# One operation for both halves of a state product, over four array tiles and two PSUM banks

## The chip, the cores and the metric

The kernel runs on one core of one Trainium2 chip. The metric is device time in microseconds (us). Before the change the median of three runs is 1085.53 us; the three lie from 1074.02 to 1090.18 us.

## What is computed

The first stage is a recurrent attention over 4 batches, 8 heads, 768 steps and head size 40. Its output, 3072 rows of 320, goes through two dense blocks.

```python
for t in range(S):
    y[:, :, t] = np.einsum('bhd,bhde->bhe', rt, state)
    Sa = np.einsum('bhde,bhe->bhd', state, at)
    state_decay = state * wt[:, :, None, :] - np.einsum('bhd,bhe->bhde', Sa, bt)
    state = state_decay + np.einsum('bhd,bhe->bhde', vt, kt)
...
h = np.maximum(np.maximum(x @ w1, x @ w2), x @ w3)
x = h @ w_out
...
return (x @ w_a) * (x @ w_b) @ w_out2
```

## The kernel before

**The work.** The 768 steps are cut into 24 chunks of 32, and the chunks into 12 pairs. `prep(p)` makes a pair's decay products (L396, L400), scaled keys (L404), and the inverse of a small triangular matrix (`solve`, on VectorE and GpSimd, with round trips through DRAM whose last ones are the transfers TT<-TD and NB<-ED). `chain(c)` carries the state through one chunk, on TensorE in this order:

- `z` (L618), the chunk's right-hand sides from the old state; ScalarE copies the result out (L624);
- `h` (L632) and `u` (L645), the two steps of the triangular solution. Each has 32 matmuls of 32 by 32 by 40, on four array tiles in turn (partitions 32j of the operands to partitions 32j of the result). `h` needs TT, `u` needs NB. ScalarE copies `u`'s result into the tile XX in four pieces (L655) and into XU (L656);
- the **state product** `smm` (L665), which this change touches. It has two halves, x = 0 and x = 1. A half's operands lie in partitions 64x to 64x+63 of the tiles YR (keys) and XX (values); its 16 matmuls (8 values of u, 2 of g) write to partitions 64g to 64g+39 of one PSUM bank. So a half uses two array tiles, g = 0 and g = 1, in turn, and each half has a bank of its own;
- in chunks 1 to 8 each half stands behind a **held product** (L673): a matmul with the identity that puts the old state into the bank first, so that ScalarE only copies the sum out (L679). In the other chunks VectorE adds the bank to the state tile ST (L682). Every fourth chunk VectorE then also scales ST (L686). ScalarE copies the new state into ZR (L693), from which the next `z` reads. The last chunk has no state product;
- transposes (L578, L594, L699), `g` (L711) and `y` (L729), which make the chunk's outputs.

float32 matmuls such as these show as two MATMUL rows each in the profile; the matmuls of the dense blocks show as one.

When a pair's outputs are there, `moe_a(p)` runs the first dense block on them (L837, eight matmuls to an operation, and L862 to L866). After the last pair, `moe_b` runs the second dense block (L991 to L1001).

**What sets the order.** All of this is given to a planner (`Plan`) as operations with an estimated duration, the tiles that each reads and writes, a priority and the number of PSUM banks that it takes (`ps`). The planner places the operations one by one on the engines, and the order that results is the program of each engine; an engine then works through its own program in that order. An operation can only be placed when as many of the eight banks are free as it names. The state product's entries are 0.82 for each half, with an activity (`act`) of 0.22. The planner also keeps a model of how busy TensorE is and where it finds too little work it puts in **fillers**, 128-column matmuls with the identity into a free bank (L277) whose result nobody reads. They serve to keep TensorE's clock up.

Of the kernel before, what the change touches and what calls it, by code (L numbers as in the profile page):

```python
# [17 lines left out]
NCH = S // C  # L18
# [7 lines left out]
NACC = 9  # L26
# [23 lines left out]
class Plan:  # L50
# [8 lines left out]
    def op(self, eng, dur, fn, r=(), w=(), ps=(), fin=(), pri=0.0, lat=None, after=(), pre=0.0, cls=0, alt=(), act=1.0, bias=None):  # L59

        i = len(self.ops)
        deps = set(after)
        for k in r:
            if k in self.lw:
                deps.add(self.lw[k])
        for k in w:
            if k in self.lw:
                deps.add(self.lw[k])
            deps.update(self.rd.get(k, ()))
        for k in r:  # L70
            self.rd.setdefault(k, []).append(i)
        for k in w:
            self.lw[k] = i
            self.rd[k] = []
        deps.discard(i)
        ways = {eng: (dur, fn, 0.0)}
        ways.update({e: (d, f, bias if bias is not None else 0.0 if pri < BIASP else BIAS) for e, d, f in alt})
        self.ops.append(dict(i=i, ways=ways, bias=bias, deps=deps, ps=tuple(ps), fin=tuple(fin), pri=pri, lat=lat, pre=pre, cls=cls, act=act))
        return i
# [159 lines left out]
def body(nc, tc, ia, out_ap):  # L239
    from contextlib import ExitStack  # L240

    V, A, G, T, SP = nc.vector, nc.scalar, nc.gpsimd, nc.tensor, nc.sync
    es = ExitStack()
    P = Plan(8)
    op = P.op
    npair = NP

    def dv(n, ps=False):
        return 0.15 + n * 0.00105 if ps else 0.12 + n * 0.0014

    def ac(n):
        return 0.17 + n * 0.0009
# [14 lines left out]
    bank = [psp.tile([128, 512], F32, name=f"bank{i}") for i in range(8)]  # L267
# [7 lines left out]
    con = cst.tile([128, 192], F32, name="con")  # L275
    ident = con[:, 0:128]
# [40 lines left out]
    ST = ap_.tile([128, 8, 2, 64], F32, name="ST")  # L317
# [223 lines left out]
    def chain(c):  # L541
        p, cc = divmod(c, 2)
        b, kb_ = p % NPB, p % 2
        z, z2, yb = c % NZR, (c + 1) % NZR, c % NYR
        pr = 0.001 * c
# [27 lines left out]
        for hf in range(2):  # L573
            pn = ("a", "yt", c, hf)
# [7 lines left out]
            for x in range(2):  # L582
# [3 lines left out]
                   r=[pn], w=[("YRy", yb, x, hf)], fin=[pn] if x else (), pri=0.5 + 0.001 * c)  # L586

        if c:
            for hf in range(2):
                pn = ("a", "st", c, hf)  # L590
# [7 lines left out]
                for i in range(2):  # L598
# [3 lines left out]
                       r=[pn], w=[("YRs", yb, 1 - i, hf)], pri=0.3 + 0.001 * c)  # L602
# [3 lines left out]
                       r=[pn], w=[("YRs2", yb, 1 - i, hf)], fin=[pn] if i else (), pri=0.3 + 0.001 * c)  # L606
# [3 lines left out]
        def zmm(w_):  # L610
# [11 lines left out]
           r=[(k, b, g, cc) for k in ("Za", "Zk") for g in range(2)] + [("ZRs", z, g) for g in range(2)] + [("ZRv", z, g) for g in range(2)],  # L622
           w=[pz], ps=[pz], pri=pr)
# [31 lines left out]
                own.append(op("ACT", ac(320), lambda w_, o_=o_, i_=i_: A.activation(o_(), i_(w_), AF.Copy), r=[pu], w=[("XXu", x, pq)], pri=pr))  # L655
        op("ACT", ac(320), lambda w_: A.activation(XU.rearrange("p b g d -> p (b g d)"), bank[w_[pu]][:, 0:320], AF.Copy), r=[pu], w=["XU"], fin=[pu], pri=pr, after=own)  # L656

        for x in range(2):
            pn = ("a", "s", c, x)

            def smm(w_, early, x=x, pn=pn):
                ps = bank[w_[pn]]
                for u in range(8):
                    for g in range(2):
                        T.matmul(ps[64 * g:64 * g + 40, u * 40:u * 40 + 40],  # L665
                                 Y_[64 * x:64 * x + 64, x, u, g], XX[64 * x:64 * x + 64, u, g], start=not early, stop=True, skip_group_check=early)

            if c == NCH - 1:
                continue
            early = 0 < c < NACC  # L670
            if early:

                op("PE", 0.6, lambda w_, x=x, pn=pn: T.matmul(bank[w_[pn]][0:104, 0:320], ident[0:104, 0:104], ST[0:104, :, 1 - x, 0:40], start=True, stop=False, skip_group_check=True),  # L673
                   r=["ST", ("STx", x), "con"], w=[pn], ps=[pn], act=0.9, pri=pr)
            op("PE", 0.82, lambda w_, smm=smm, early=early: smm(w_, early), r=[("YRy", yb, x, hf) for hf in range(2)] + [("XXu", x, pq) for pq in range(2)] + [("XXv", x)],
               w=[pn], ps=[] if early else [pn], act=0.22, pri=pr)
            sv = ST[0:104, :, 1 - x, 0:40]
            if early:
                op("ACT", ac(320), lambda w_, sv=sv, pn=pn: A.activation(sv, bank[w_[pn]][0:104, 0:320].rearrange("p (u d) -> p u d", d=40), AF.Copy),  # L679
                   r=[pn], w=["ST", ("STx", x)], fin=[pn], pri=pr)  # L680
            else:
                op("DVE", dv(320, True), lambda w_, sv=sv, pn=pn: V.tensor_tensor(  # L682
                    sv, bank[w_[pn]][0:104, 0:320].rearrange("p (u d) -> p u d", d=40), sv, ALU.add),
                   r=[pn], w=["ST", ("STx", x)], fin=[pn], pri=pr)
            if cc and p % 2:
                op("DVE", 0.74, lambda w_, sv=sv, x=x: V.tensor_tensor(  # L686
                    sv, sv, P_[0:104, cc].rearrange("p (u x) s -> p u x s", x=2)[:, :, x, 32:33].to_broadcast([104, 8, 40]), ALU.mult),
                   r=pc, w=["ST", ("STx", x)], pri=pr)
            for g in range(2):
                r0 = GP[g]  # L690
                o_ = ZR[z2][r0:r0 + 40, g, :, 1 - x]
                i_ = ST[r0:r0 + 40, :, 1 - x, 0:40]
                op("ACT", ac(320), lambda w_, o_=o_, i_=i_: A.activation(o_, i_, AF.Copy), r=[("STx", x)], w=[("ZRs", z2, g)], pri=pr)  # L693
# [3 lines left out]
        def xtr(w_):  # L697
# [6 lines left out]
            r=[px], w=[("XTu", 0), ("XTu", 1)], fin=[px], pri=0.2 + pr)  # L704
# [9 lines left out]
        for x in range(2):  # L714
# [4 lines left out]
               r=[pg, "con"], w=[("YLg", x)], fin=[pg] if x else (), pri=0.2 + pr)  # L719
        py = ("a", "y", c)  # L720

        def ymm(w_):
# [14 lines left out]
           r=[py] + pc, w=[("XY", cc), "cxa", "cxb", "cxf"], fin=[py], pri=0.2 + pr)  # L737
# [305 lines left out]
    for p in range(npair):  # L1043
        a0 = len(P.ops)
        chain(2 * p)
        chain(2 * p + 1)
        if p + 2 < npair:
            prep(p + 2)
        gather(p)
        att.extend(range(a0, len(P.ops)))  # L1050
        a0 = len(P.ops)
        moe_a(p)
        ma.extend(range(a0, len(P.ops)))
# [218 lines left out]
```

## Time and profile before

| what | us |
|---|---|
| runs, lowest / median / highest | 1074.02 / 1085.53 / 1090.18 |
| span of the profiled execution, first to last instruction | 1092.1 |
| TensorE busy in it | 1045.6 (96%) |
| VectorE busy | 639.8 (59%) |
| ScalarE busy | 499.3 (46%) |

The profiled execution has no time of its own beside its span; it is 6.6 us above the median of the runs and 1.9 us above the highest. Engines: PE is TensorE's matmuls, PEld its weight loads, DVE VectorE, ACT ScalarE, POOL GpSimd, SP the engine that issues most transfers. PEclk is the share of TensorE's full clock that was granted; the clock has two levels, 1.2 and 2.4 GHz, so 0.90 over a stretch means a fifth of it at the lower level. A busy PE is not one at its peak: a pipelined matmul's row is longer than the time until the next one starts.

### The profile page before, as it was taken

The numbers are of one execution on the slowest core, as the hardware profiler recorded it, in microseconds if no ns is written. First come the engines' busy times: TensorE is split into PE (matmuls) and PEld (weight loads), VectorE is DVE, ScalarE is ACT, GpSimd is POOL, SyncE is SP. The second block draws the span as 40 slices with busy tenths as digits, with TensorE's granted clock in tenths as the row PEclk, the third lists the DMA queues.
The fourth block names the chain that finished last, engine by engine and source line by source line (L and its number), as shares of the span: only waits on it lengthen the run. The fifth ranks groups of instructions, "written<-read, shape, count | busy, mean of one in ns | idle before, by whom it ended". The sixth has DMA issues, their size and how long they took to land.

```text
span 1092.1 us, 34136 instructions
## 1 busy us (share of the span) xinstructions
PE 1045.6 (96%) x14792; PEld 938.5 (86%) x14792; DVE 639.8 (59%) x1035; ACT 499.3 (46%) x1157; POOL 252.2 (23%) x212
## 2 busy tenths in 40 slices
PE   8999799999989999899999999999999999999997
PEld 7888687878889888789899999988888888888886
DVE  7796797696778787787877333376223232332222
ACT  5357664576656467474756522243222232222221
POOL 3332555343336625441413000011000000000000
PEclk9899896989999989999999999999999999999999
DMA  8757874867666677857555239522002000000000
GB/s 266 178 128 165 184 171 105 175 138 189 171 165 169 151 167 199 184 134 184 132 140 131 55 103 274 131 78 61 22 1 54 1 25 1 1 25 1 25 1 27
DMA packets 173436, 123.08 MB, mean 113 GB/s; under 512 B 122464, under 2 KB 147168, under 8 KB 172320
## 3 DMA queue, kind: packets, MB, share of 16 engines
q1 hardware_dynamic: 170688, 116.41, 43.3%
q10 hardware_dynamic: 2592, 4.42, 1.1%
q8 instruction: 118, 1.93, 0.8%
q14 instruction: 38, 0.31, 0.1%
HBM read 93.07 MB, written 27.72 MB: 111 GB/s over the span
## 4 chain that ended last, share of the span: by engine, by line
PE 56%; DVE 2%; DMA 2%; issue 1%; SPq 1%; ACT 0%; POOL 0%; ACTq 0%; DVEq 0%; POOLq 0%
PE bank L991 24%; PE bank L837 10%; PE bank L999 4%; PE bank L1000 4%; PE bank L1001 4%; PE bank L665 1%; PE bank L862 1%; PE bank L729 1%; PE bank L711 1%; PE bank L864 1%; PE bank L863 1%; PE bank L594 1%; PE bank L645 1%; PE bank L632 1%; PE bank L429 1%
## 5 line engine op out<-in xcount | busy, mean ns | idle before, releaser
L1009 DVE TENSOR_TENSOR bas<-bank,bas 128x512 f32<-128x512 f32 x72 | 49.8, 691 | 194.1 <-PE bank L991 185.3
L991 PE MATMUL bank<-bxhi,bw 128*128 128x512 f32 x576 | 156.3, 393 | 0.0
L991 PEld LDWEIGHTS bank<-bxhi,bw 128*128 128x128 f32 x576 | 106.0, 188 | 20.6
L1008 ACT ACTIVATE bas<-bank 128x512 f32<-128x512 f32 x72 | 43.0, 598 | 143.1 <-PE bank L991 143.0
L1011 ACT ACTIVATE bgh<-bas 128x512 fp32r<-128x512 f32 x72 | 45.6, 633 | 132.4 <-DVE bas L1009 132.4
L837 PE MATMUL bank<-xhi,whi 128*128 128x256 f32 x432 | 97.6, 309 | 0.2 <-issue 0.2
L991 PE MATMUL bank<-bxlo,bw 128*128 128x512 f32 x288 | 89.7, 393 | 0.0
L837 PE MATMUL bank<-xhi,wlo 128*128 128x256 f32 x432 | 89.6, 290 | 0.0
L837 PE MATMUL bank<-xlo,whi 128*128 128x256 f32 x432 | 89.3, 289 | 0.0
L999 PE MATMUL bank<-bo,bgh 128*128 128x320 f32 x288 | 88.9, 309 | 0.0
L1001 PE MATMUL bank<-bo,bgl 128*128 128x320 f32 x288 | 88.9, 309 | 0.0
L1000 PE MATMUL bank<-bo,bgh 128*128 128x320 f32 x288 | 88.8, 308 | 0.0
L852 DVE TENSOR_TENSOR hm<-bank,hm 128x512 f32<-128x512 f32 x72 | 49.5, 687 | 63.3 <-PE bank L837 59.7
L414 POOL TENSOR_TENSOR ZL<-ZL,Pp 64x512 f32<-64x512 f32 x44 | 59.8, 1360 | 88.6 <-DVE Pp L396 69.9
L1012 DVE TENSOR_TENSOR bgl<-bas,bgh 128x512 fp32r<-128x512 f32 x72 | 50.7, 705 | 42.8 <-ACT bgh L1011 42.6
L837 PEld LDWEIGHTS bank<-xhi,whi 128*128 128x128 f32 x432 | 68.9, 198 | 5.3 <-DVE wraw L760 1.6
L837 PEld LDWEIGHTS bank<-xhi,wlo 128*128 128x128 f32 x432 | 69.8, 198 | 0.0
L837 PEld LDWEIGHTS bank<-xlo,whi 128*128 128x128 f32 x432 | 69.8, 198 | 0.0
L991 PEld LDWEIGHTS bank<-bxlo,bw 128*128 128x128 f32 x288 | 54.1, 188 | 12.3
L837 PE MATMUL bank<-xt,wt 128*128 128x256 f32 x216 | 62.3, 288 | 0.8 <-issue 0.8
L837 PE MATMUL bank<-xl,wt 128*128 128x256 f32 x216 | 62.1, 287 | 0.0
L277 PE MATMUL bank<-con 128*128 128x128 f32 x386 | 57.2, 301 | 3.4 <-DMA con<-in_con_dram 2.8
(183 smaller groups left out, 2488.5 us busy)
## 6 DMA issues: line engine op xcount, KB each, us to landing
wraw<-in_wpb_dram SPq DMA_DIRECT2D x18, 480.0 KB
KT<-in_kb_dram SPq DMA_DIRECT2D x20, 384.0 KB
Pp<-in_wf_dram SPq DMA_DIRECT2D x10, 528.0 KB
Rp<-in_wr_dram SPq DMA_DIRECT2D x10, 528.0 KB
wraw<-in_wpa_dram SPq DMA_DIRECT2D x12, 384.0 KB
bw<-WD SPq DMA_DIRECT2D x9, 512.0 KB
WD<-wraw ACTq DMA_DIRECT2D x18, 240.0 KB
WD<-wca SPq DMA_DIRECT2D x18, 240.0 KB
```

What stands on the lines that cost most here:

```text
L277: P.keep = lambda b: T.matmul(bank[b][:, 0:128], ident, ident, start=True, stop=True)
L414: op("POOL", po(512), lambda w_, cc=cc, g=g, r0=r0: G.tensor_tensor(Z_[r0:r0 + 64, cc, g], Z_[r0:r0 + 64, cc, g], P_[r0:r0 + 64, cc, :, 0: ...
L837: T.matmul(ps, w, x, start=(i == 0), stop=(i == 7))
L852: op("DVE", dv(512, True), lambda w_, pn=pn: V.tensor_tensor(f(hm), bank[w_[pn]], f(hm), ALU.max), r=[pn], w=["hm"], fin=[pn], pri=ep)
L991: T.matmul(ps, w, x, start=(k == 0), stop=(k == 7))
L999: T.matmul(o, gh[:, c], oh, start=ff == 0, stop=False)
L1000: T.matmul(o, gh[:, c], ol, start=False, stop=False)
L1001: T.matmul(o, gl[:, c], oh, start=False, stop=ff == 11)
L1008: op("ACT", ac(512), lambda w_, j=j, pa=pa: A.activation(tb["as", j], bank[w_[pa]], AF.Copy), r=[pa], w=[("bas", j)], fin=[pa], pri=ep)
L1009: op("DVE", dv(512, True), lambda w_, j=j, pb=pb: V.tensor_tensor(tb["as", j], bank[w_[pb]], tb["as", j], ALU.mult), r=[pb], w=[("bas", j) ...
L1011: op("ACT", ac(512), lambda w_, j=j, k=k: A.activation(tb["gh", k], tb["as", j], AF.Copy), r=[("bas", j)], w=[("gh", k)], pri=ep)
L1012: op("DVE", dv(512), lambda w_, j=j, k=k: V.tensor_tensor(tb["gl", k], tb["as", j], tb["gh", k], ALU.subtract), r=[("bas", j), ("gh", k)], ...
```

## The change

The two halves become one operation of 32 matmuls. Its loops run over u, then x, then g, so that consecutive matmuls go to (x, g) = (0,0), (0,1), (1,0), (1,1): four array tiles in turn, the x = 0 ones into the first bank and the x = 1 ones into the second. It reads what both halves read, and takes both banks at once. The two held products become one operation as well. What the planner is told changes: 0.9 for the whole product with an activity of 0.4, and 1.2 for both held products. The copies and sums behind it (L679 to L693) stay one per half; lines from L679 on are two higher in the changed kernel.

```diff
-        for x in range(2):
-            pn = ("a", "s", c, x)
-
-            def smm(w_, early, x=x, pn=pn):
-                ps = bank[w_[pn]]
-                for u in range(8):
+        pss = [("a", "s", c, x) for x in range(2)]
+        early = 0 < c < NACC
+
+        def smm(w_):
+            for u in range(8):
+                for x in range(2):
                     for g in range(2):
-                        T.matmul(ps[64 * g:64 * g + 40, u * 40:u * 40 + 40],
+                        T.matmul(bank[w_[pss[x]]][64 * g:64 * g + 40, u * 40:u * 40 + 40],
                                  Y_[64 * x:64 * x + 64, x, u, g], XX[64 * x:64 * x + 64, u, g], start=not early, stop=True, skip_group_check=early)
...
-                op("PE", 0.6, lambda w_, x=x, pn=pn: T.matmul(bank[w_[pn]][0:104, 0:320], ident[0:104, 0:104], ST[0:104, :, 1 - x, 0:40], start=True, stop=False, skip_group_check=True),
-                   r=["ST", ("STx", x), "con"], w=[pn], ps=[pn], act=0.9, pri=pr)
-            op("PE", 0.82, lambda w_, smm=smm, early=early: smm(w_, early), r=[("YRy", yb, x, hf) for hf in range(2)] + [("XXu", x, pq) for pq in range(2)] + [("XXv", x)],
-               w=[pn], ps=[] if early else [pn], act=0.22, pri=pr)
+                op("PE", 1.2, held, r=["ST", ("STx", 0), ("STx", 1), "con"], w=pss, ps=pss, act=0.9, pri=pr)
+            op("PE", 0.9, smm, r=[("YRy", yb, x, hf) for x in range(2) for hf in range(2)] + [("XXu", x, pq) for x in range(2) for pq in range(2)] + [("XXv", x) for x in range(2)],
+               w=pss, ps=[] if early else pss, act=0.4, pri=pr)
```

Since the planner places everything anew, the whole program's order moves, not only these operations. The number of fillers goes from 193 to 257, that of all other matmuls stays. By chunk (counted by the `z` they stand behind; -1 is ahead of the first), the fillers stand so: -1 to 3, 147 before and 171 after; 4, 11 and 42; 5 to 22, 23 and 32; 23, 12 and 12. Behind the last `z` stand 432 matmuls of L837 before and 408 after.

TensorE's program around the state product of chunk 14, before (XX holds the values, YR the keys; L699 is a transpose; L866 and L837 are of the first dense block):

```order
L865 MATMUL bank_65<-hhi,woh 128x256
L866 MATMUL bank_65<-hlo,woh 128x256
L665 MATMUL bank_70<-XX,YR_131 40x40 x16
L699 MATMUL bank_68<-con,XU 80x128 x4
L665 MATMUL bank_67<-XX,YR_131 40x40 x16
L837 MATMUL bank_64<-xhi,whi 128x256 x2
```

And the same place after (L839 is L837 of before):

```order
L839 MATMUL bank_69<-xlo,whi 128x256 x2
L839 MATMUL bank_69<-xt_109,wt_103 128x256
L839 MATMUL bank_69<-xl_110,wt_103 128x256
L665 MATMUL bank_65<-XX,YR_131 40x40 x2
L665 MATMUL bank_68<-XX,YR_131 40x40 x2
```

The last two rows come eight times in turn, and the transpose (now L701) follows them: nothing stands between the halves any more.

TensorE's program in chunk 4, from behind `h` to the first half of the state product, before (L447 is `prep`'s product of keys, ZL and KT its tiles):

```order
L447 MATMUL bank_64<-ZL_126,KT_125 64x32 x32
L837 MATMUL bank_70<-xhi,whi 128x256 x2
L837 MATMUL bank_70<-xhi,wlo 128x256 x2
L837 MATMUL bank_70<-xlo,whi 128x256 x2
L837 MATMUL bank_70<-xt_109,wt_103 128x256
L837 MATMUL bank_70<-xl_110,wt_103 128x256
L277 MATMUL bank_63<-con 128x128 x5
L447 MATMUL bank_63<-ZL_126,KT_125 64x32 x32
L645 MATMUL bank_65<-Zy,NB_144 32x40 x32
L277 MATMUL bank_67<-con 128x128 x5
L665 MATMUL bank_69<-XX,YR_131 40x40 x16
```

And after, from `h`:

```order
L632 MATMUL bank_66<-Zs,TT_141 32x40 x32
L578 MATMUL bank_65<-con,KT_124 128x104 x4
L277 MATMUL bank_64<-con 128x128 x27
L447 MATMUL bank_64<-ZL_126,KT_125 64x32 x32
L277 MATMUL bank_66<-con 128x128 x14
L645 MATMUL bank_66<-Zy,NB_144 32x40 x32
L447 MATMUL bank_69<-ZL_126,KT_125 64x32 x32
L839 MATMUL bank_70<-xhi,whi 128x256 x2
```

The first dense block, which stood between these operations, now first comes behind `u`, and fillers stand in its place.

VectorE's program around the two sums into the state in chunk 13, before (L503 is part of `solve`, TC and TP its tiles):

```order
L682 TENSOR_TENSOR ST<-bank_67,ST 104x8x40
L503 TENSOR_REDUCE TC<-TP_149 128x4x8
L682 TENSOR_TENSOR ST<-bank_70,ST 104x8x40
L503 TENSOR_REDUCE TC<-TP_150 128x4x8
L852 TENSOR_TENSOR hm<-bank_68,hm 128x512
```

And after, with L684 for L682, L717 for the masking of `g`'s result and L400 of the next `prep`:

```order
L503 TENSOR_REDUCE TC<-TP_150 128x4x8
L684 TENSOR_TENSOR ST<-bank_69,ST 104x8x40
L684 TENSOR_TENSOR ST<-bank_67,ST 104x8x40
L717 TENSOR_TENSOR YL<-bank_66,con 64x512 x2
L400 SCALAR_TENSOR_TENSOR Rp<-Rp,d_96 128x528
```

The two sums now stand one behind the other.

## Rows read from the trace of the kernel before

**Rows 1.** The page: span, TensorE's busy time, its clock in 40 slices
```profile
span 1092.1 us, 34136 instructions
PE 1045.6 (96%) x14792; PEld 938.5 (86%) x14792; DVE 639.8 (59%) x1035; ACT 499.3 (46%) x1157; POOL 252.2 (23%) x212
...
PEclk9899896989999989999999999999999999999999
```

**Rows 2.** Busy time by stage: the stretch, its length, then each engine's busy us
```profile
core 0: us, PE busy (x) PEld busy (x) DVE busy (x) ACT busy (x) POOL busy (x), PEclk, DMA share, GB/s
0.00:133.00 133.00, 122.11 (x2240) 102.73 (x2244) 103.32 (x185) 76.26 (x199) 49.99 (x45) 0.94 0.75 185
133.00:500.00 367.00, 339.44 (x7236) 309.91 (x7240) 287.65 (x459) 224.99 (x564) 165.50 (x133) 0.92 0.68 162
500.00:609.00 109.00, 107.13 (x2310) 100.14 (x2297) 82.79 (x136) 64.18 (x156) 27.70 (x23) 1.00 0.54 138
609.00:691.00 82.00, 82.00 (x1003) 80.49 (x1002) 29.58 (x47) 24.66 (x52) 1.45 (x2) 1.00 0.57 158
691.00:1092.00 401.00, 394.94 (x2038) 345.25 (x2036) 136.47 (x212) 109.16 (x189) 7.58 (x10) 1.00 0.10 28
```

**Rows 3.** Groups of TensorE's instructions by line: count, busy us, mean ns, idle before
```profile
L665 PE MATMUL bank<-XX,YR 64*40 64x40 f32 x1472 | 39.8, 210 | 2.3 <-issue 1.8 <-ACT XX L655 0.5
L632 PE MATMUL bank<-Zs,TT 32*32 32x40 f32 x1536 | 24.0, 204 | 11.0 <-DMA TT<-TD 6.5 <-issue 4.1
```

**Rows 4.** The chain of waits, pieces from four stretches: start us, us, what
```profile
413.81 0.74 PE bank L665 x32
...
418.94 0.73 PE bank L618 x62
...
606.30 1.23 PE bank L665 x63
...
611.81 0.72 PE bank L632 x64
...
642.62 1.34 PE bank L277 x12
...
665.38 0.96 PE bank L837 x8
```

**Rows 5.** Instructions in order of time around chunk 14's state product
```profile
411.75 1.79 ACT L655 ACTIVATE XX<-bank 32x320 f32<-32x320 f32 x4 [1.58 <-PE bank L645]
...
413.74 0.81 PE L665 MATMUL bank<-XX,YR 64*40 64x40 f32 x32
...
414.60 0.49 DVE L682 TENSOR_TENSOR ST<-bank,ST 104x320 f32<-104x320 f32 x1 [0.94 <-PE bank L665]
...
415.05 0.81 PE L665 MATMUL bank<-XX,YR 64*40 64x40 f32 x32
...
416.17 0.47 DVE L682 TENSOR_TENSOR ST<-bank,ST 104x320 f32<-104x320 f32 x1
...
417.16 0.95 ACT L693 ACTIVATE ZR<-ST 40x320 f32<-40x320 f32 x2
```

**Rows 6.** TensorE in order of time: chunk 0's `h`, and fillers in chunk 4
```profile
60.74 0.50 PE L789 MATMUL bank<-wraw,con 64*64 64x192 f32 x2
61.17 0.89 PE L632 MATMUL bank<-Zs,TT 32*32 32x40 f32 x64
...
149.05 1.28 PE L277 MATMUL bank<-con 128*128 128x128 f32 x10
150.26 2.06 PE L447 MATMUL bank<-ZL,KT 40*64 40x32 f32 x64
152.24 0.79 PE L645 MATMUL bank<-Zy,NB 32*32 32x40 f32 x64
152.96 1.38 PE L277 MATMUL bank<-con 128*128 128x128 f32 x10
```

**Rows 7.** Busy time of the fillers alone (L277), the first stretch
```profile
0.00:133.00 133.00, 43.98 (x294) 40.38 (x294) 0.94 0.75 185
```

More of the change, by code (lines that the diff above doesn't have):

```diff
@@ L656, in chain, with held @@
         op("ACT", ac(320), lambda w_: A.activation(XU.rearrange("p b g d -> p (b g d)"), bank[w_[pu]][:, 0:320], AF.Copy), r=[pu], w=["XU"], fin=[pu], pri=pr, after=own)
-        for x in range(2):
-            pn = ("a", "s", c, x)
-            def smm(w_, early, x=x, pn=pn):
-                ps = bank[w_[pn]]
-                for u in range(8):
+        pss = [("a", "s", c, x) for x in range(2)]
[3 more added lines that the diff above has]
+                for x in range(2):
                     for g in range(2):
-                        T.matmul(ps[64 * g:64 * g + 40, u * 40:u * 40 + 40],
+                        T.matmul(bank[w_[pss[x]]][64 * g:64 * g + 40, u * 40:u * 40 + 40],
                                  Y_[64 * x:64 * x + 64, x, u, g], XX[64 * x:64 * x + 64, u, g], start=not early, stop=True, skip_group_check=early)
-            if c == NCH - 1:
-                continue
-            early = 0 < c < NACC
+        def held(w_):
+            for x in range(2):
+                T.matmul(bank[w_[pss[x]]][0:104, 0:320], ident[0:104, 0:104], ST[0:104, :, 1 - x, 0:40], start=True, stop=False, skip_group_check=True)
+        if c < NCH - 1:
             if early:
-                op("PE", 0.6, lambda w_, x=x, pn=pn: T.matmul(bank[w_[pn]][0:104, 0:320], ident[0:104, 0:104], ST[0:104, :, 1 - x, 0:40], start=True, stop=False, skip_group_check=True),
-                   r=["ST", ("STx", x), "con"], w=[pn], ps=[pn], act=0.9, pri=pr)
-            op("PE", 0.82, lambda w_, smm=smm, early=early: smm(w_, early), r=[("YRy", yb, x, hf) for hf in range(2)] + [("XXu", x, pq) for pq in range(2)] + [("XXv", x)],
-               w=[pn], ps=[] if early else [pn], act=0.22, pri=pr)
+                op("PE", 1.2, held, r=["ST", ("STx", 0), ("STx", 1), "con"], w=pss, ps=pss, act=0.9, pri=pr)
+            op("PE", 0.9, smm, r=[("YRy", yb, x, hf) for x in range(2) for hf in range(2)] + [("XXu", x, pq) for x in range(2) for pq in range(2)] + [("XXv", x) for x in range(2)],
+               w=pss, ps=[] if early else pss, act=0.4, pri=pr)
+        for x in range(2 if c < NCH - 1 else 0):
+            pn = pss[x]
             sv = ST[0:104, :, 1 - x, 0:40]
```

## Prediction

> **What bounds the kernel now.** I read the page first. TensorE is busy for 1045.6 us of a span of 1092.1 us, and no other engine for more than 59% of it [rows 1]. A sum over stages with different limits does not say what one of them is worth, so the second view is the busy time by stage [rows 2]. From 691 us to the end the second dense block runs alone at the full clock; nothing there is touched. From 609 to 691 us the chain of chunks has made its last state, and TensorE is busy for all of the 82.00 us: the first dense block's backlog is worked off. That is the key to this case. What ends the first part is not the chain but the amount of work in TensorE's program, so a microsecond saved on TensorE before 609 us comes off the end, as long as it does not turn into idle time there. From 133 to 609 us TensorE is busy for 339.44 + 107.13 = 446.57 of 476 us, idle for 29.4 us. Its clock costs about as much: 0.92 over 367 us is 0.08 x 367 = 29 us of full-speed time. From 0 to 133 us there is no backlog yet, the chain waits for `prep` and its transfers, and 294 of the 386 filler rows stand there [rows 7].
>
> **The product itself.** A half of the state product holds TensorE for 0.74 us (32 rows, 16 matmuls), and two halves back to back for 1.23 us [rows 4]. Twenty of the 23 chunks have something between the halves, three have not; so now the product costs 20 x 1.48 + 3 x 1.23 = 33.3 us. How long four tiles in turn take for this shape no row of the trace shows. Below, the nearest is `h`, four tiles in turn with the same 40 columns to stream: 64 rows in 0.72 us; `z`, whose four tiles lie in different columns of the array over all of its rows, needs 0.73 us for 62 [rows 4]. Above, the halves just follow each other as now, 1.48 us; further still, `prep`'s product of keys, two tiles in turn, needs 2.06 us for 64 rows, with 64 instead of 40 result rows [rows 6], which would make the product 0.58 us slower than two halves. I take 0.75 us, near `h` and `z`: the trace shows that the time per row goes from 0.74/32 = 23 ns with two tiles to 0.72/64 = 11 ns with four, as if each tile had a fixed time per matmul and the tiles ran side by side. What is new here, two tiles that share array columns and differ in rows, is what keeps the upper bound alive. **Term 1: 33.3 - 23 x 0.75 = 16.0 us less** (bounds: 33.3 - 23 x 0.72 = 16.7 less; 23 x 2.06 - 33.3 = 14.1 more).
>
> The Trainium skill speaks against this: "TensorE: Matmul & The Clock Gate", section "Wait — 56ns, not 53.3ns?", gives a floor of about 25 ns from one matmul's start to the next, however few the columns. By it 64 rows could not take less than 1.6 us, and term 1 would be nil. This trace does not agree: `h` has 64 rows in 0.72 us [rows 4].
>
> **The held products** keep their two matmuls in each of eight chunks; putting them together moves nothing off TensorE. Zero; were they delayed by needing both parts of the state and two banks at once, the fillers and dense work ahead of them would cover it.
>
> **The fillers.** 64 more than before. Twelve filler rows, six matmuls, take 1.34 us [rows 4], so one takes 0.223 us and 64 take 14.3 us at the full clock: nearly all of term 1. A filler costs nothing where TensorE would have waited. Three places, three answers. Ahead of chunk 4 there are 24 more, 5.4 us. There fillers stand ahead of operations that wait for transfers, but chunk 0's `h` follows the work ahead of it without a gap [rows 6], so the wait was just covered or over-covered. I take half, 2.7 us. In chunk 4 there are 31 more, 6.9 us, where six operations of the first dense block stood before; that work (48 matmuls at 0.96/8 = 0.12 us [rows 4], 5.8 us) is done later, out of the backlog that ends at 691 us. So these cost in full. The other nine cost 2.0 us in full. **Term 2: 2.7 + 6.9 + 2.0 = 11.6 us more** (bounds 0 and 14.3).
>
> **The chain.** The product can now only start when all four copies into XX are done. Around chunk 14 these end at 411.75 + 1.79 = 413.54 us, and the first half starts at 413.74, after them already [rows 5]; the dense work ahead of it hides that wait, and uncovered it would be two copies, 0.9 us a chunk. Behind the product VectorE's sums now follow one another: 0.49 + 0.47 us after a product that ends at about 413.74 + 0.75 = 414.5 us, so at 415.6 us with the 0.1 us of signalling; before, the second sum ended at 416.17 + 0.47 = 416.64. The state is there 1.0 us earlier where something stood between the halves, and at the same time where nothing did. I count it at zero, since the end waits for TensorE's work and not for the chain; queued behind the second sum on VectorE is `g`'s masking, which is not later. Multiplications that change between VectorE and GpSimd are off the path in a stretch where VectorE is busy for 287.65 of 367 us [rows 2].
>
> **Sum.** -16.0 + 11.6 = -4.4 us on the span of 1092.1 us, 1087.7 us. The order agrees in kind: 24 fewer matmuls of the dense block are left behind the last `z`, 24 x 0.12 = 2.9 us. The runs' median stands 6.6 us below the profiled span, so the forecast is 1085.5 - 4.4 = **1081 us**.
>
> **The rivals.**
>
> - *The fillers are free.* If in the new order every added filler stands where TensorE would have waited, only term 1 is left: 1085.5 - 16.0 = 1069.5 us. For it: 11.0 us of idle time stand ahead of `h`, mostly for TT [rows 3], so there are waits to fill. Against it: in chunk 4 the fillers stand in place of real work. If the denser product also holds the clock up where it fell (0.92, [rows 2]) and gives back 6 to 10 of those 29 us, it is about 1061 us. Chance 0.2, half of it for the part past 2%.
> - *The rotation gains nothing, and the fillers stay.* This is the case on the other side. Its place is the product's 64 rows, its mechanism that two tiles in the same columns of the array cannot run side by side, and its price the 11.6 us of fillers: 1085.5 + 11.6 = 1097 us, and 1100 us if all 14.3 count; three halves that were already back to back change that by under a microsecond. It decides from the point where the product takes more than (33.3 - 11.6)/23 = 0.94 us. For it: no row shows such a pair. Against it: no row shows TensorE's time per row staying at 23 ns with four tiles. The Trainium skill's floor of the page named above would come to the same time. Chance 0.13.
> - *The clock.* Between 133 and 500 us TensorE loses about 29 us to the lower level, in slices that the page shows at 6 and 8 tenths [rows 1]. A new order moves these. The product's shorter run leaves more of the chain's thin operations next to each other; if a third more is lost than now, 10 us, the time is 1091 us, and with three quarters more, 22 us, 1103 us. Against it: the fillers are there to prevent just this. Chance 0.12.
>
> **How the numbers follow.** The forecast has 0.55, the rivals 0.2, 0.13 and 0.12. The range has to reach the free fillers, and a little past them, at the low end, 1065 us, and the no-gain case at the high end, 1100 us. Faster by over 2% means under 1063.8 us: only half of the first rival, 0.1, and a little for a forecast whose order turns out luckier, 0.02: 0.12. Slower by over 2% means over 1107.2 us: the worst of the clock rival and the 2.06 us bound, 0.08. The rest, 0.80, is within 2%, about what a measurement of this kernel can tell from no change: the three runs of before lie 1.5% apart.
>
> **What would show it.** In the profile after, L665 should have 1472 rows as now, but a piece of 64 should last 0.72 to 0.8 us; 1.2 us or more means that the tiles do not run side by side. L277 should have 514 rows. The stage from the last `z` to the second dense block should be some 3 us shorter than 82 us. PEclk between 133 and 500 us should stay near 0.92, and PE's idle time there near 30 us: if idle time grows by what the product saves, the gain was turned into waiting and my reading that TensorE's work sets the end is wrong. If the first dense block starts much later than before, the time went into the stretch ahead of it, which I took as nearly unchanged. A second dense block that is not about 401 us long would mean that something else differs.

## The result, and the profile after

The changed kernel takes 1093.23 us (median of 20 runs, 1085.36 to 1104.39). The kernel before, in 20 runs beside it, takes 1082.62 us (1074.02 to 1094.34). The ratio is 1.0094, with an interval of 1.0073 to 1.0116: 0.9% or 10 us slower. The ratios leave out single runs that lie over 1.5% above the fastest of their kernel: here one of the changed kernel's 20 (1104.39 us), further on one each of e10 and e13, and one of e4 that took 1925.59 us. The forecast was 4.4 us faster. The time lies in the range and within 2%, but the sign is wrong.

The page of the changed kernel, the lines of [rows 1]:

```profile
span 1092.2 us, 34405 instructions
...
PE 1038.1 (95%) x14920; PEld 933.2 (85%) x14920; DVE 648.9 (59%) x1040; ACT 501.1 (46%) x1157; POOL 243.8 (22%) x207
...
PEclk9889798899999998999999999999999999999999
```

Beside [rows 1] there seems to be no difference at all: 1092.2 against 1092.1 us. But that execution of before lay some 10 us above the median of its runs. Profiled again (e9 below), the same kernel has a span of 1082.3 us, so both are used here.

The groups of TensorE's instructions after (columns as in [rows 3]: count, busy us, mean ns, idle before):

```profile
L277 PE MATMUL bank<-con 128*128 128x128 f32 x514 | 69.5, 291 | 2.9 <-DMA con<-in_con_dram 2.9
L632 PE MATMUL bank<-Zs,TT 32*32 32x40 f32 x1536 | 23.0, 207 | 7.2 <-issue 4.8 <-DMA TT<-TD 2.1
L665 PE MATMUL bank<-XX,YR 64*40 64x40 f32 x1472 | 20.4, 205 | 0.8 <-issue 0.3 <-DMA XX<-in_vx_dram 0.3 <-ACT XX L655 0.2
...
L670 PE MATMUL bank<-ST,con 104*104 104x320 f32 x32 | 11.4, 474 | 1.2 <-DVE ST L684 1.2
```

The product's 1472 rows took 39.8 us [rows 3] and now take 20.4 (L670 is the held products). One whole product, in the chain of waits of after (start us, us, what):

```profile
413.48 0.76 PE bank L665 x64
...
613.10 0.76 PE bank L665 x64
```

So 64 rows need 0.76 us, where 32 needed 0.74 [rows 4]: two tiles that share columns of the array and differ in rows do run side by side. Around chunk 14, in order of time:

```profile
413.41 0.82 PE L665 MATMUL bank<-XX,YR 64*40 64x40 f32 x64
...
414.27 0.89 DVE L684 TENSOR_TENSOR ST<-bank,ST 104x320 f32<-104x320 f32 x2
...
415.33 1.94 ACT L695 ACTIVATE ZR<-ST 40x320 f32<-40x320 f32 x4
```

From the product's start to the copies into ZR it is 1.92 us, where it was 417.16 - 413.74 = 3.42 [rows 5]. All that the change does directly is there, as it was meant. What it costs must lie elsewhere. By stage (columns as in [rows 2]):

```profile
0.00:133.00 133.00, 116.69 (x2026) 97.44 (x2030) 100.04 (x171) 64.82 (x168) 45.49 (x43) 0.90 0.71 175
133.00:500.00 367.00, 342.17 (x7622) 314.46 (x7614) 303.00 (x476) 237.64 (x593) 159.38 (x131) 0.95 0.67 162
500.00:609.00 109.00, 102.06 (x2133) 95.47 (x2134) 81.34 (x137) 62.78 (x152) 29.88 (x22) 0.98 0.60 150
609.00:691.00 82.00, 82.00 (x1119) 80.31 (x1118) 27.79 (x45) 26.66 (x56) 1.46 (x2) 1.00 0.57 158
691.00:1092.00 401.00, 395.18 (x2040) 345.50 (x2038) 136.72 (x212) 109.24 (x189) 7.59 (x10) 1.00 0.10 28
```

TensorE waits more in the first stretch (16.3 us against 10.9 of [rows 2]) and from 500 to 609 us (6.9 against 1.9), and a little less between. The first dense block starts at 168.0 us, where it started at 134.6. TensorE in order of time at that place, first before, then after:

```profile
134.55 0.77 PE L837 MATMUL bank<-xhi,whi 128*128 128x256 f32 x2
```

```profile
167.98 0.79 PE L839 MATMUL bank<-xhi,whi 128*128 128x256 f32 x2
```

And the last `z`, before and after:

```profile
609.36 0.84 PE L618 MATMUL bank<-ZR,ZL 128*32 128x40 f32 x51
```

```profile
617.25 0.80 PE L618 MATMUL bank<-ZR,ZL 128*32 128x40 f32 x64
```

The tail from the last `z` to the second dense block became 7.6 us shorter (82.1 to 74.5), but the last `z` comes 7.9 us later; the block starts at 691.5 and 691.8 us.

**Where the product's 18 us went.** The kernel before, profiled again (e9): its span with the mean clock, TensorE's busy time up to its second dense block (count in brackets, then PEclk, DMA share, GB/s), and the groups of its fillers and its product.

```profile
core 0: 1082.3 us, clock 0.976
```

```profile
0.00:681.50 681.50, 640.57 (x12761) 0.96 0.67 164
```

```profile
L277 PE MATMUL bank<-con 128*128 128x128 f32 x386 | 57.2, 301 | 3.7 <-DMA con<-in_con_dram 2.8 <-DVE ZL L454 0.9
L665 PE MATMUL bank<-XX,YR 64*40 64x40 f32 x1472 | 38.2, 207 | 1.3 <-issue 1.3
```

The same span and stretch of the changed kernel:

```profile
core 0: 1092.2 us, clock 0.967
```

```profile
0.00:691.80 691.80, 643.72 (x12889) 0.95 0.65 162
```

Up to the second dense block TensorE is busy for 643.72 - 640.57 = 3.15 us more and idle for 48.08 - 40.93 = 7.15 us more: together the 10.3 us by which the block is later. Within the busy time the product gives 17.8 us (38.2 - 20.4), the fillers take 12.3 of them (69.5 - 57.2), and the remaining work, the same matmuls, takes 8.65 us longer. At those mean clocks 26.0 and 36.0 us are lost to the lower level: that is about this amount. The clock is the unsure part. The two executions of the kernel before, 0.965 and 0.976, are 12 us apart in it, while their idle times up to 691 and 681.5 us agree (40.3 by [rows 2], and 40.9). From single profiles only the idle time and the fillers are sure to differ.

The runs settle the clock, since each has its mean granted clock on record. It is 0.975 on average over the 91 runs of the kernel before that stand beside the experiments, and 0.972 over 19 of the changed kernel. One minus the clock, times the span, is an estimate of what the lower level cost: 27.0 and 30.4 us. So some 3 us of the 10 are the clock (the uncertainty is about 2 us), and 7 are not.

The new idle time stands ahead of `z` (L618) and `u` (L645), which waits for the transfer NB<-ED of the inverse. First before (e9), then after:

```profile
L645 PE MATMUL bank<-Zy,NB 32*32 32x40 f32 x1536 | 22.5, 200 | 6.2 <-DMA NB<-ED 3.3 <-issue 2.7
L618 PE MATMUL bank<-ZR,ZL 128*32 128x40 f32 x1536 | 19.8, 205 | 0.0
```

```profile
L645 PE MATMUL bank<-Zy,NB 32*32 32x40 f32 x1536 | 24.8, 208 | 9.4 <-DMA NB<-ED 8.6 <-issue 0.6
L618 PE MATMUL bank<-ZR,ZL 128*32 128x40 f32 x1536 | 22.6, 213 | 9.6 <-issue 7.2 <-DMA ZR<-in_vz_dram 2.0 <-DVE YL L717 0.3
```

### The profile page after: what moved, and what is told of

It is laid out like the page before. It is cut to its first block, busy times and chain, and to the rows that moved or that the text cites. A ratio compares the mean times of both kernels' runs of the same rounds, so it can differ in the third digit from the quotient of the medians.

```text
span 1092.2 us, 34405 instructions
## 1 busy us (share of the span) xinstructions
PE 1038.1 (95%) x14920; PEld 933.2 (85%) x14920; DVE 648.9 (59%) x1040; ACT 501.1 (46%) x1157; POOL 243.8 (22%) x207
## 4 chain that ended last, share of the span: by engine, by line
PE 67%; DVE 14%; DMA 8%; issue 4%; SPq 3%; ACT 2%; POOL 1%; DVEq 0%; ACTq 0%; POOLq 0%
PE bank L993 24%; PE bank L839 11%; PE bank L1001 4%; PE bank L1003 4%; PE bank L1002 4%; PE bank L277 2%; PE bank L731 2%; DVE TP L502 2%; DMA ED<-TC 2%; DVE Pp L396 2%; PE bank L618 1%; DMA NB<-ED 1%; PE bank L713 1%; DVE hm L854 1%; PE bank L594 1%
## 5 line engine op out<-in xcount | busy, mean ns | idle before, releaser
L839 PE MATMUL bank<-xhi,whi 128*128 128x256 f32 x432 | 97.4, 308 | 0.1
L854 DVE TENSOR_TENSOR hm<-bank,hm 128x512 f32<-128x512 f32 x72 | 49.4, 686 | 69.5 <-PE bank L839 58.2
L839 PE MATMUL bank<-xlo,whi 128*128 128x256 f32 x432 | 89.2, 289 | 0.6 <-DVE xlo L828 0.6
L839 PE MATMUL bank<-xhi,wlo 128*128 128x256 f32 x432 | 89.2, 289 | 0.0
L277 PE MATMUL bank<-con 128*128 128x128 f32 x514 | 69.5, 291 | 2.9 <-DMA con<-in_con_dram 2.9
L839 PEld LDWEIGHTS bank<-xhi,whi 128*128 128x128 f32 x432 | 68.8, 198 | 3.5 <-DVE XY L735 0.3
L839 PEld LDWEIGHTS bank<-xlo,whi 128*128 128x128 f32 x432 | 69.4, 197 | 0.8 <-DVE xlo L828 0.8
L839 PEld LDWEIGHTS bank<-xhi,wlo 128*128 128x128 f32 x432 | 69.6, 198 | 0.0
L277 PEld LDWEIGHTS bank<-con 128*128 128x128 f32 x514 | 64.7, 203 | 5.5 <-ACT bank L345 2.9
L993 PEld LDWEIGHTS bank<-bxlo,bw 128*128 128x128 f32 x288 | 54.1, 188 | 12.3
L839 PE MATMUL bank<-xt,wt 128*128 128x256 f32 x216 | 62.4, 289 | 0.0
```

Source lines behind the costliest of these rows:

```text
L277: P.keep = lambda b: T.matmul(bank[b][:, 0:128], ident, ident, start=True, stop=True)
L839: T.matmul(ps, w, x, start=(i == 0), stop=(i == 7))
L854: op("DVE", dv(512, True), lambda w_, pn=pn: V.tensor_tensor(f(hm), bank[w_[pn]], f(hm), ALU.max), r=[pn], w=["hm"], fin=[pn], pri=ep)
L993: T.matmul(ps, w, x, start=(k == 0), stop=(k == 7))
```

## Experiments

Each ratio is that of the runs to runs of the kernel before beside them, with its interval.

**1. The order.** Theory O: the planner's new order costs the time, the product itself gains. Rival C: the product's gain is lost in the chain of chunks whatever the order. e1 leaves every engine's order as it was before, with its 193 fillers, and puts the whole product, in rotation, at the place of the first half, or as soon behind it as the copies that it reads are listed.

```diff
-            fn(where)
+            self.seq.append(i)
+            o["fn"] = fn
...
+            deps[s0] |= deps[s1]
+            ps[s0] = ps[s0] + ps[s1]
+            fn[s0] = g["sfn"]
+            alias[s1] = s0
```

> The kernel before with its order kept on every engine (193 fillers, VectorE, GpSimd, ScalarE and the transfers in the same order); only the two halves are put together at the place of the first half (or as soon as the copies it reads are listed), in rotation over four tiles, and the two held products likewise. Order theory (the loss of the changed kernel comes from the new order that the planner made, the merged product itself helps): 10 to 17 us faster than before, about 1067 to 1073 us beside 1083. Chain theory (the product was not on the path, or putting it together delays the sums): within 3 us of before. Product theory (the merged product itself costs the time): 5 to 12 us slower than before.

Measured: 1078.26 us, 0.9947 [0.9919, 0.9976], 5.7 us faster than before. Less than theory O asked for, more than C allowed. Its product and held products:

```profile
L768 PE MATMUL bank<-XX,YR 64*40 64x40 f32 x1472 | 23.1, 207 | 10.0 <-issue 5.7 <-DMA XX<-in_vx_dram 1.9 <-DVE XY L816 1.3
...
L773 PE MATMUL bank<-ST,con 104*104 104x320 f32 x32 | 12.8, 520 | 2.9 <-DVE ST L751 2.9
```

The saving of 15.1 us (38.2 to 23.1) is there; 8.7 us of new idle time stand ahead of the product (10.0 against 1.3), and 2.9 ahead of the held ones. That it comes from both parts having to be ready at the first half's place is argued: most of it has no releaser in the trace ("issue"). The change is worth something, and the order that the planner makes (fillers included) decides whether one sees it: 1.5% lie between e1 and the changed kernel.

**2. The rotation alone.** e2 is the changed kernel, whose order and fillers stay, with x as the outermost loop, so that the halves follow each other; e7 is e1 with the same edit.

```diff
-            for u in range(8):
-                for x in range(2):
+            for x in range(2):
+                for u in range(8):
```

> The changed kernel in its own order, but the loop over x outermost in the product: the same 32 matmuls, two tiles in turn for the first half, then two for the second. The product should take 1.23 us for 64 rows instead of 0.76. If TensorE's work sets the end: 23 x 0.47 = 11 us slower than the changed kernel, about 1104 us. If waits take up what the product saves: within 3 us of the changed kernel.

> The old order kept and the halves put together as in the first experiment, but one half behind the other, two tiles in turn (1.23 us instead of 0.76). Work theory: 23 x 0.47 = 11 us slower than with the rotation, 1089 us. Wait theory (what the rotation saves turns into waits and lower clock): within 3 us of it, about 1078 to 1081, and then the gain of the first experiment comes from putting the halves together, not from the rotation.

Measured: e2 1093.12 us, 1.0101 [1.0061, 1.0142]; e7 1083.34 us, 1.0005 [0.9971, 1.0038]. The product's group and the busy time up to the second dense block in e2, then the group in e7 with a piece of its chain of waits:

```profile
L665 PE MATMUL bank<-XX,YR 64*40 64x40 f32 x1472 | 31.5, 207 | 0.0
```

```profile
0.00:690.40 690.40, 648.94 (x12888) 0.96 0.66 162
```

```profile
L768 PE MATMUL bank<-XX,YR 64*40 64x40 f32 x1472 | 32.4, 205 | 5.3 <-issue 2.5 <-DVE XY L816 1.7 <-ACT ST L744 0.9
```

```profile
567.65 1.23 PE bank L768 x63
```

Without the rotation two halves need 1.23 us, with it 0.76. In the old order the rotation saves 9.3 us of product (32.4 to 23.1), and e1 is 0.6% faster than e7, some 6 us (the intervals meet between 0.9971 and 0.9976). In the changed kernel's order it saves 11.1 us (31.5 to 20.4), and the times are the same: idle time there goes from 41.5 to 48.1 us, and the mean clock of the profile from 0.974 to 0.967 (over the runs from 0.974 to 0.972). So in that order 11.1 us of TensorE's work cost nothing that the time shows, and e2's second alternative, that waits take up what the product saves, came true; e7 lies between its two. Putting the halves together without the rotation gives nothing (e7).

**3. The fillers.** e3 is the changed kernel with at most as many fillers behind each `z` as before (182 instead of 257; where its own order has fewer, none are added).

```diff
+    def keep(b):
+        given[at[0]] = given.get(at[0], 0) + 1
+        if given[at[0]] <= most.get(at[0], 0):
+            T.matmul(bank[b][:, 0:128], ident, ident, start=True, stop=True)
```

> The changed kernel in its own order, with at most as many fillers in each chunk as the kernel before has (182 in all instead of 257). Filler theory: 75 x 0.223 = up to 17 us faster than the changed kernel, and chunk 1's z at about 75 us as before instead of 85. Order theory: chunk 1's z stays at about 85 us, since the triangular solution of the first pair ends 7 us later on VectorE; the time changes by less than 5 us, or grows where the clock falls without the fillers.

Measured: 1087.16 us, 1.0060 [1.0029, 1.0091]: 0.34% or 3.7 us of the changed kernel's loss come back, of the 75 x 0.223 = 16.7 us that they would be in full. Fillers, and busy time up to its second dense block:

```profile
L283 PE MATMUL bank<-con 128*128 128x128 f32 x364 | 50.5, 295 | 2.8 <-DMA con<-in_con_dram 2.8
```

```profile
0.00:682.70 682.70, 629.45 (x12738) 0.95 0.66 164
```

The idle time becomes 53.2 us, 5.1 more than in the changed kernel. The clock falls too: 0.964 on average over e3's runs, against 0.972, which by the same estimate costs 38.9 us instead of 30.4, 8.5 us more. So the fillers hold TensorE for most of their time, but give about half of it back as clock. What is left, 3.7 us, is about a third of the loss; the two intervals meet, so it could be anything from nothing to some 8 us.

**4. The start.** An early difference lies ahead of any product, in VectorE's part of the first pair's inverse. Its last reduction and the transfer behind it, before and after:

```profile
54.70 1.26 DVE L503 TENSOR_REDUCE TC<-TP 128x32 f32<-128x512 f32 x2
55.98 1.09 SPq L482 DMA_DIRECT2D ED<-TC  x2
```

```profile
61.52 1.26 DVE L503 TENSOR_REDUCE TC<-TP 128x32 f32<-128x512 f32 x2
62.83 1.23 SPq L482 DMA_DIRECT2D ED<-TC  x2
```

Chunk 0's `h` starts at 66.05 us, where it started at 61.17 [rows 6]. The theory was that these early microseconds are the loss. e5 takes the changed kernel and gives it before's order up to chunk 1's `z` alone (238 fillers); e6 takes the changed kernel's order up to there and before's behind it (212).

```diff
+            for k, i in enumerate(other.seq):
+                if i is None:
+                    fill.append((0, k))
+                elif i in to:
+                    key[to[i]] = (0, k)
+                    eng[to[i]] = other.ops[i]["eng"]
+                if i == other.mark["z1"]:
+                    break
```

> The changed kernel's operations; up to chunk 1's z in the order that the kernel before has on every engine, from there in the changed kernel's order, with its fillers (238 in all). Theory of the early loss (the changed kernel loses its 10 us ahead of chunk 1's z, by the new order of VectorE and GpSimd there, and keeps that offset): chunk 1's z at 72 to 76 us instead of 85, and 7 to 12 us faster than the changed kernel, about 1081 to 1086. Theory of the late loss (the order behind it is as bad, or the start's gain is spent in waits later): within 4 us of the changed kernel.

> The reverse: up to chunk 1's z in the changed kernel's order, from there in the order of the kernel before, with the merged product (212 fillers). Theory of the early loss: chunk 1's z at 82 to 86 us, and 7 to 12 us slower than the run with the old order kept throughout, about 1085 to 1090. Theory of the late loss: within 4 us of that run, about 1078.

Measured: e5 1090.58 us, 1.0082 [1.0044, 1.0121]; e6 1090.96 us, 1.0092 [1.0053, 1.0130]. In e5 chunk 1's `z` starts at 72.2 us (changed kernel 85.3), and still the first dense block starts late:

```profile
161.82 0.79 PE L949 MATMUL bank<-xhi,whi 128*128 128x256 f32 x2
```

So the early loss is real in the trace and not what the time is made of. e6 by itself would have fitted the theory (12.7 us above e1), but e5 does not, and the theory falls. Nor is the rest of the order alone to blame, since e6, with that rest as before, is 1.4% slower than e1. Each piece of the new order costs about as much as the whole.

**5. What a microsecond on TensorE is worth.** e8 is e1 with the product done three times in chunks 0 and 9 to 22, 30 products more.

```diff
+                    for k in range(1 if early else 3):
                         for u in range(8):
```

> The old order kept, merged and in rotation, but in chunks 0 and 9 to 22 the product is made three times over into the same banks (the second and third overwrite the first with the same values): 15 x 2 x 0.76 = 22.8 us more work on TensorE, all of it on the way to the next state. Work theory: 20 to 23 us slower than with the product once, about 1100 us. Wait theory: under 12 us slower.

Measured: 1129.37 us, 1.0437 [1.0375, 1.0499], 51 us above e1. The group, and one place in order of time:

```profile
L769 PE MATMUL bank<-XX,YR 64*40 64x40 f32 x3392 | 44.5, 206 | 33.6 <-issue 29.1 <-DMA XX<-in_vx_dram 2.3 <-DVE XY L817 1.6
```

```profile
544.85 1.19 PE L769 MATMUL bank<-XX,YR 64*40 64x40 f32 x99
547.15 1.12 PE L769 MATMUL bank<-XX,YR 64*40 64x40 f32 x93 [1.12 <-issue]
```

TensorE is held for more than the rows: a gap of 1.12 us opens within the three. With such gaps it is held for (44.5 + 33.6) - (23.1 + 10.0) = 45.0 us more, and the time grows by 51; the mean clock of the runs, 0.967 against e1's 0.973, accounts by the same estimate for about the rest (7.7 us). Neither alternative had foreseen the gaps. Writing the same two banks over again does not by itself open them: one writing is 64 rows, this gap stands behind 99, another behind 145, and in one chunk all 192 rows pass without a gap. e1, which writes them once, has such a gap too, 2.18 us behind 61 rows. First from e8, then from e1:

```profile
69.35 1.61 PE L769 MATMUL bank<-XX,YR 64*40 64x40 f32 x145
72.19 0.67 PE L769 MATMUL bank<-XX,YR 64*40 64x40 f32 x47 [1.24 <-issue]
...
561.32 2.05 PE L769 MATMUL bank<-XX,YR 64*40 64x40 f32 x192
```

```profile
474.46 0.86 PE L768 MATMUL bank<-XX,YR 64*40 64x40 f32 x61
477.49 0.35 PE L768 MATMUL bank<-XX,YR 64*40 64x40 f32 x3 [2.18 <-issue]
```

What opens them stays open ("issue"). Here the added time counts in full; it is added to TensorE's work and to the chain at once, and this run cannot tell the two apart. It is no rule: e2's 11.1 us more than the changed kernel did not count, and of what e1 took away 5.7 of 15.1 us did.

**6. Other orders of both kernels.** If an order is worth more than the product, orders that come from nearly the same numbers must scatter. e4, e10, e11 and e16 are the kernel before with another number told to the planner; e12 to e15 the changed kernel; e9 is the kernel before unchanged. The numbers have no other effect than the order and the number of fillers.

```diff
-            op("PE", 0.82, lambda w_, smm=smm, early=early: smm(w_, early), r=[("YRy", yb, x, hf) for hf in range(2)] + [("XXu", x, pq) for pq in range(2)] + [("XXv", x)],
+            op("PE", 0.8, lambda w_, smm=smm, early=early: smm(w_, early), r=[("YRy", yb, x, hf) for hf in range(2)] + [("XXu", x, pq) for pq in range(2)] + [("XXv", x)],
```

(e10: 0.84; e16: 0.9; e11: `act` 0.4 for 0.22.) In the changed kernel:

```diff
-                op("PE", 1.2, held, r=["ST", ("STx", 0), ("STx", 1), "con"], w=pss, ps=pss, act=0.9, pri=pr)
+                op("PE", 0.6, held, r=["ST", ("STx", 0), ("STx", 1), "con"], w=pss, ps=pss, act=0.9, pri=pr)
```

(That is e12. e13: the same, and 0.82 and 0.22 for the product; e14: 0.82 for 0.9; e15: `act` 0.22 for 0.4.)

> The kernel before, with one number changed: the planner is told 0.80 instead of 0.82 for each half of the state product. No instruction changes, only the order. Order theory: the time moves by some 5 to 15 us either way, though nothing was added or removed. If order is not worth that much: within 3 us of before.

> The kernel before, unchanged, for another profile of it: the first one's span, 1092.1 us, lies 9.5 us above the median of its runs. Expected: a span near 1083 us, and, ahead of the second dense block, less idle time or less time at the lower clock than the 40.3 and 75.1 us of the first profile, since the work is the same.

> The kernel before with the planner told 0.84 instead of 0.82 for each half. No instruction is added or removed but fillers (217 instead of 193). If the order of the kernel before is a lucky one among many: 0.5 to 1.6% slower than before, as with 0.80. If the number 0.80 was just a bad one: within 0.4% of before.

> The kernel before with the planner told an activity of 0.4 instead of 0.22 for each half, the duration unchanged (204 fillers). The order stays the same at first and then goes its own way. Lucky-order theory: 0.5 to 1.6% slower than before. Otherwise: within 0.4%.

> The changed kernel with the planner told 0.6 instead of 1.2 for the two held products (239 fillers); all operations as in the changed kernel. Lucky-order theory: another draw, 0.5% faster to 1.5% slower than before, on average 0.5% better than the draws of the unchanged product. If the changed kernel's loss came from the merged product: 0.9% slower than before, as it is.

> The changed kernel with the planner told what one half was before: 0.6 for the held products, 0.82 and an activity of 0.22 for the product (246 fillers). If the merged product gains on average over orders: between 1% faster and 1.2% slower than before, below the 1.4 to 2.2% of the three draws of the unchanged product. If the draw of 1.0% faster was luck: 1.4 to 2.2% slower.

> The changed kernel with the planner told 0.82 instead of 0.9 for the product (260 fillers). Same alternatives: between 1% faster and 1.2% slower than before, or 1.4 to 2.2% slower.

> The changed kernel with the planner told an activity of 0.22 instead of 0.4 for the product (247 fillers). Same alternatives: between 1% faster and 1.2% slower than before, or 1.4 to 2.2% slower.

> The kernel before with the planner told 0.90 instead of 0.82 for each half (216 fillers). If the order of before is a selected one: 1.4 to 2.2% slower than before, as the other three draws. Otherwise within 0.8%.

The last column is the estimate of above, one minus the mean clock of the runs times their span; for the kernel before it is 27.0 over its 91 runs.

| kernel | told | fillers | us | ratio | lost to the lower clock, us |
|---|---|---|---|---|---|
| two halves (before) | 0.82, act 0.22 (e9) | 193 | 1082.94 | 1.0001 [0.9959, 1.0042] | 25.4 |
| two halves | 0.80 (e4) | 199 | 1100.66 | 1.0144 [1.0085, 1.0202] | 39.7 |
| two halves | act 0.4 (e11) | 204 | 1102.56 | 1.0189 [1.0143, 1.0234] | 38.7 |
| two halves | 0.84 (e10) | 217 | 1104.10 | 1.0218 [1.0177, 1.0260] | 33.9 |
| two halves | 0.9 (e16) | 216 | 1109.28 | 1.0228 [1.0181, 1.0276] | 43.3 |
| one product | held 0.6 (e12) | 239 | 1071.11 | 0.9899 [0.9851, 0.9946] | 23.3 |
| one product | held 0.6, 0.82, act 0.22 (e13) | 246 | 1088.99 | 1.0051 [1.0019, 1.0083] | 30.3 |
| one product | 0.82 (e14) | 260 | 1088.01 | 1.0052 [1.0018, 1.0085] | 27.7 |
| one product | 0.9, held 1.2, act 0.4 (changed) | 257 | 1093.23 | 1.0094 [1.0073, 1.0116] | 30.4 |
| one product | act 0.22 (e15) | 247 | 1095.09 | 1.0139 [1.0095, 1.0182] | 37.2 |

A step of 0.02 us in one number, with the same work but for 6 and 24 fillers, makes the kernel before 1.4 to 2.2% slower (e4, e10). Of the 16 to 25 us that the four other orders cost, 7 to 16 us are lower clock and 3 to 15 us are not. Its own order is the best of the five tried for two halves. The changed kernel's orders lie from 0.9899 to 1.0139, and their mean is 1.0047; the four other orders of two halves have a mean of 1.0195, and 1.0156 with before's own. The difference, 1.1 to 1.5% or 12 to 16 us, has term 1's size. But the orders of either kernel scatter by about 0.9%, so with five of each the 1.1% is uncertain by some 1.3% and not clear of nothing. e13 and e14 came out as a gain over orders would have it, e15 at the edge of the other alternative; an order that wins by chance is not excluded. What the whole product gains at one and the same order is shown by e1 alone, 0.5%.

e12 beats both kernels, by 1.0% and 1.9%. Its span with the mean clock, and its busy time up to the second dense block:

```profile
core 0: 1072.4 us, clock 0.978
```

```profile
0.00:673.00 673.00, 630.47 (x12866) 0.97 0.66 162
```

It has 18 fillers fewer than the changed kernel, 42.5 us of idle time instead of 48.1, and a mean clock of 0.978 in its profile and its runs (the changed kernel: 0.967 and 0.972). What it is told is no better estimate: the held pair is put down at 0.6 us, while in the changed kernel the eight pairs keep TensorE busy for 11.4 us (L670), 1.4 us each.

## Why the prediction was wrong, point by point

- **What bounds the kernel** was half right. That TensorE's work ahead of 609 us sets the end holds in e8 (51 us for 45 added, on the chain as well). It does not hold in general: e1 kept 5.7 of 15.1 us taken away, and in the changed order 11.1 us more or less make no difference (e2). The condition stood in the sentence, "as long as it does not turn into idle time there", and was not priced.
- **Term 1** was right: 0.76 us against 0.75, so 33.3 - 23 x 0.76 = 15.8 us for 16.0. The rival that the rotation gains nothing is false in its mechanism, though its 1097 us lies nearer to the measured time than the forecast. The floor of about 25 ns from one matmul's start to the next ("TensorE: Matmul & The Clock Gate" of the Trainium skill, "Wait — 56ns, not 53.3ns?") is again not what the runs show: 64 rows in 0.76 us are 12 ns a row.
- **The held products** at zero: 1.2 us of idle time in the changed kernel, 2.9 in e1. Near enough.
- **Term 2** left out what fillers give back. Taking 75 out gives 3.7 us (e3), so 64 cost about 3 us and not 11.6. As time on TensorE the price was not far off: without the 8.5 us that e3 lost to the clock, the 75 would have given some 12 to 13 us of their 16.7. But fillers that "cost in full" also hold the clock up, which the term did not count, though a rival names it.
- **The chain.** Forecast was 1.0 us less from the product's start to the end of the second sum. Measured are 2.90 us before [rows 5] and 1.75 after, 1.15 us less (1.5 us to the copies into ZR). It brought nothing that the time shows; that it was off the path all along is not shown.
- **The sum** is the step that failed: "The order agrees in kind". The rest of the new order was put down as nothing, with the dense matmuls behind the last `z` as its only check. That check came true (7.6 us shorter, for 3) and meant nothing, as the last `z` moved by as much. By the runs the sum is: 5.7 us faster for the product with the order kept (e1), 3.7 us slower for the fillers (e3), and the rest of the way to 10 us slower, some 12 us, for the order (each known to some 3 to 4 us). It is a price of the size that the kernel before pays when its own order, with its fillers, is drawn again (1.4 to 2.3%, 16 to 25 us), if somewhat less. In the trace it shows as waits ahead of `z` and `u`, and over the runs as a slightly lower clock.
- **The clock rival** (10 us more lost, 1091 us) is nearest in time, mostly by luck. By the clocks of the runs the changed kernel loses 3.4 us more to the lower level and not 10: a third of the loss. The 10 us that the profile of after loses more than e9 are one execution each, and e1, with the same mean clock in its profile, 0.967, is 15 us faster.
- **What would show it.** The late first dense block was named as a warning, and came (168.0 us). PEclk from 133 to 500 us did not fall (0.95), nor did idle time there grow; the waits are in the stretches on either side.

**What stays open.** Which places of before's order make it better by 1.4 to 2.3% than its neighbours. Ahead of `z`, `h` and `u` TensorE is idle for 15.5 and 16.5 us together in the two profiles of the kernel before, and for 20.9 to 29.7 us in those of the nine other orders that the planner made; but e12, the fastest, has 26.5, so this alone is not it. Exchanging the part up to chunk 1's `z`, or the part behind it, finds no single place (e5, e6). Nor was a longer row of orders tried, from which a chance that a given order wins could be said.

## What to carry to other kernels

Where a planner sets the whole program's order, a change of one operation is two changes, the operation and a new draw of the order; measure the operation in the old order, and draw the old kernel's order a few times by small steps in its numbers, before believing either sign. Time taken off the busiest engine is worth its full length only if what stands behind it is ready; price the condition, with the idle time that each operation already has ahead of it. A filler has two prices, the time that it takes and the clock that it holds: count both. A profile is one execution: two of the same kernel differed by 10 us with the same idle time and another clock, so compare idle time and work, and the runs' medians and clocks, before reading a difference of spans.

## What the runs showed of the hardware

- Four array tiles in turn, of which two and two share columns and differ in rows, with a bank for each row half, run as fast as the other four tiles here: 64 rows of 64 x 40 in 0.76 us (`h`: 0.72 us [rows 4]), against 1.23 us for 63 when the same matmuls go two tiles at a time.
- Writing the same two banks three times over directly one behind the other cost nothing at 561.32 us of e8: 192 rows in 2.05 us without a gap. Gaps in its other chunks stand in the middle of a writing, and the trace names no releaser for them.
- 75 fillers fewer, with nothing else changed, took the mean granted clock over the runs from 0.972 to 0.964 (e3).
